# Retention into a gated feed-forward block on one core: a gap behind each head of v, and a new order of loads and transposes for chunks 2 and 3

## The chip, the cores and the metric

The kernel runs on one core of a Trainium2 chip. The metric is the device time in microseconds. TensorE (PE) multiplies matrices, VectorE (DVE), ScalarE (ACT) and GpSimd (POOL) work on elements, and SyncE (SP) issues transfers. POOL issues transfers too; both queues end on the same 16 DMA engines.

## The reference

Four batches of eight heads go through a retention recurrence, and its output, laid out as 3072 tokens of 512, through an RMS norm and a gated feed-forward block:

```
B, H, S, D = 4, 8, 768, 64
for t in range(S):
    state = gamma[h] * state + outer(k[:, :, t], v[:, :, t])
    y[:, :, t] = (1 / sqrt(D)) * q[:, :, t] @ state
x   = y.transpose(0, 2, 1, 3).reshape(B * S, H * D)
xn  = x / sqrt(mean(x * x) + 1e-6) * rms_g
out = (silu(xn @ w_gate) * (xn @ w_val)) @ w_out        # 512 -> 1536 -> 512
```

## The kernel before, in words

The 768 steps are cut into six chunks of 128. In a chunk, a **unit** is one batch: 128 steps on the partitions, eight heads of 64 in the free dimension; two units make a **pair**. The recurrence becomes matrix work: scores `a_ps` from the transposed k and q (`a_pe`, L485; `a_pair` does both units of a pair), a causal mask on DVE (`a_mask`, L494), values `y_ps` from masked scores and from the running state (`values`, L514 and L531), and the chunk's contribution to the state (`kv_ps`, L523; added on DVE by `state_add`). The decays are put on v beforehand (`vp`, L468, on POOL) and on y afterwards (`y_out`, L440, on DVE). Then come the squares (`square`, L449, on ACT), the inverse root (`rstd`, L454 and L370, on POOL), the norm (`norm`, L462, on DVE) and a transpose of the normed rows into `xnT`.

The feed-forward part of a chunk covers its 512 tokens: `gv` (L560) multiplies by the two input weights into PSUM, ACT takes the silu (L564), DVE the product `hT` (L565); `down` (L579) multiplies by the output weight, ACT copies to `o_sb` (L581), SP stores it. Chunks 0 and 1 use a layout of their own for the attention part (pairs of steps, `load_pair`, `tp`, `ap`, `y0`, `y1`, L300 for the weighting of v), and q and k are transposed on TensorE there. From chunk 2 on, `load` fetches q and k per unit as bf16 and v as float32, all on POOL's queue (L110 for v, L113 for q and k), and `t_dma` (L476) transposes q and k by DMA transposes on SP's queue. `x_dma` (L543) transposes the normed rows there too.

Everything is written out in program order by hand: each engine takes its instructions in that order. The feed-forward of chunk c runs on PE while the attention of chunk c + 1 is prepared and put between its steps; the table `after` says which calls follow which step. In chunk 1's stage there are 12 steps of `gv` and four of `down`: the attention of chunk 2 lies inside it, and the scores of chunk 3's first pair (`values(2, 1, (3, 0), True)`) close step 12. The loads and transposes of chunks 2 and 3 are placed in the last part of chunk 0's stage and in chunk 1's stage.

Tiles come in rings of buffers: v of a unit has 6 (`v_f`, shared with the four exponential masks of chunk 0, `mask0`), q and k 8 each, the transposed ones 8 each, output rows 3. A load into a ring waits until the last reader of the buffer is through.

Of the kernel before, what the change touches and what calls it, by code (L numbers as in the profile page):

```python
# [8 lines left out]
F32 = mybir.dt.float32  # L9
# [7 lines left out]
def kernel(  # L17
# [14 lines left out]
    B, H, S, D = q.shape  # L32
# [12 lines left out]
    work = ctx.enter_context(tc.tile_pool(name="work", bufs=4))  # L45
# [19 lines left out]
    def bank(name, dtype=F32, ffn=False, i=None):  # L65
        if i is None and split[0]:
            i = turn[ffn] % 4 + 4 * ffn
            turn[ffn] += 1
        elif i is None and first:
            i = first.pop(0)  # L70
        elif i is None:
            i = order[0]
            order.append(order.pop(0))
        return psum.tile([128, 512 if dtype == F32 else 1024], dtype, name=name, tag=f"p{i}")
# [30 lines left out]
    def load(c, b, names="qkv"):  # L105
        u = U.setdefault((c, b), {})
        for n in names:
            if n == "v":
                x = work.tile([128, H, D], F32, name="v_f", tag="v_f", bufs=6)
                nc.gpsimd.dma_start(out=x, in_=unit_v[n][c, b])  # L110
            else:
                x = work.tile([128, DM], BF16, name=n + "b", bufs=8)
                nc.gpsimd.dma_start(out=x.rearrange("p (h d) -> p h d", h=H), in_=unit_v[n][c, b])  # L113
            u[n] = x
# [58 lines left out]
    nc.vector.tensor_scalar(out=causal, in0=off, scalar1=0.0, scalar2=None, op0=ALU.is_ge)  # L173


    mask0 = [[work.tile([128, 2, 256], F32, name="mask0", tag="v_f", bufs=6) for i in range(2)] for a in range(2)]

    def mask_exp(a):
        for i in range(2):
# [103 lines left out]
    def ap_mask(c, p, a, i):  # L283
        u = U[c, p]
        am = work.tile([128, 2, 2, 128], BF16, name="am2", tag="am", bufs=12)
        m = mask0[a][i] if c == 0 else causal_p[:, None, :].to_broadcast([128, 2, 256])
        u["mask", a, i] = nc.vector.tensor_tensor(  # L287
            out=am.rearrange("p x e t -> p x (e t)"),
            in0=u["a_ps", a][i].rearrange("p (x t) -> p x t", x=2), in1=m, op=ALU.mult)
        u["am", a, i] = am  # L290
# [6 lines left out]
    def vp_pair(c, p):  # L297
        u = U[c, p]
        x = work.tile([128, H * 2, D], BF16, name="vp2", bufs=3)
        nc.gpsimd.tensor_tensor(  # L300
            out=x, in0=u["v"].rearrange("p h (e d) -> p (h e) d", e=2),
            in1=vd_p[:, c].rearrange("p h e -> p (h e)")[:, :, None].to_broadcast([128, 2 * H, D]), op=ALU.mult)
        u["vp"] = x.rearrange("p (h e) d -> p h (e d)", e=2)
# [99 lines left out]
    def y1(p):  # L403
        u = U[1, p]
        u["y"] = [bank("y_ps") for _ in range(2)]
        for b in range(2):
            for hp in range(NHP):
                nc.tensor.matmul(u["y"][b][:, hp * 128:(hp + 1) * 128],
                                 u["qT", hp // 2][b][:, hp % 2].rearrange("p e j -> p (e j)"), st_d[p][:, b, hp],
                                 start=hp == 0, stop=False, skip_group_check=True)  # L410
        for h in range(H):
            hp, i = h // 2, h % 2
            for e in range(2):
                for b in range(2):
                    r = slice(b * 64, b * 64 + 64)
                    nc.tensor.matmul(u["y"][b][:, h * D:h * D + D], u["am", hp // 2, i][r, hp % 2, e, :],
                                     u["vp"][r, h, e * D:e * D + D], start=False,
                                     stop=h == H - 1 and e == 1, skip_group_check=True)

    def y1_out(p):  # L420
        u = U[1, p]
        x = work.tile([128, 2, NHP, 2, D], F32, name="x", tag="x", bufs=2)
        u["x"] = x.rearrange("p b a i d -> p b (a i d)")
        for b in range(2):
            nc.vector.tensor_tensor(
                out=u["x"][:, b].rearrange("p (h d) -> p h d", h=H), in0=u["y"][b].rearrange("p (h d) -> p h d", h=H),
                in1=yd_p[:, :, None].to_broadcast([128, H, D]), op=ALU.mult)
# [16 lines left out]
    def square(c, p, b):  # L444
        u = pair(c, p)
        if b == 0:
            u["ms_"] = work.tile([128, 2], F32, name="ms", bufs=4)
        xsq = work.tile([128, DM], BF16, name="xsq", bufs=2)
        nc.scalar.activation(xsq, u["x"][:, b], AF.Square, scale=1.0 / math.sqrt(DM), accum_out=u["ms_"][:, b:b + 1])  # L449
# [7 lines left out]
    def norm(c, p, *units):  # L457
        u = pair(c, p)
        if 0 in units:
            u["xn"] = [work.tile([128, DM], BF16, name="xn", bufs=6) for _ in range(2)]  # L460
        for b in units:
            nc.vector.scalar_tensor_tensor(out=u["xn"][b], in0=u["x"][:, b], scalar=u["rstd"][:, b:b + 1], in1=g_bc,  # L462
                                           op0=ALU.mult, op1=ALU.mult)
# [8 lines left out]
    def t_dma(c, b):  # L472
        u = U[c, b]
        for n in "qk":
            t = work.tile([128, NHP, 128], BF16, name=n + "T", tag=n + "T", bufs=8)
            nc.sync.dma_start_transpose(out=t, in_=u[n])  # L476
            u[n + "T"] = t
# [70 lines left out]
    def gv(c, n0, n1, t0, t1):  # L548

        if c not in HT:  # L550
            HT[c] = work.tile([128, NFF, GT], BF16, name="hT", bufs=1)
        w = t1 - t0
        m = (n1 - n0) * w
        ps = []
        for wt, name in ((wg_b, "g_ps"), (wv_b, "v_ps")):
            x = bank(name, ffn=True)
            for n in range(n0, n1):
                o = (n - n0) * w
                for s in range(KS):
                    nc.tensor.matmul(x[:, o:o + w], wt[:, s, n * 128:(n + 1) * 128], XT[c][:, s, t0:t1],  # L560
                                     start=s == 0, stop=s == KS - 1)
            ps.append(x)
        sg = work.tile([128, 512], BF16, name="sg", bufs=4)
        nc.scalar.activation(sg[:, :m], ps[0][:, :m], AF.Silu)  # L564
        return nc.vector.tensor_tensor(  # L565
            out=HT[c][:, n0:n1, t0:t1], in0=sg[:, :m].rearrange("p (n t) -> p n t", t=w),
            in1=ps[1][:, :m].rearrange("p (n t) -> p n t", t=w), op=ALU.mult)

    def store(eng, c, b, m, o_sb):
        if c < 2:  # L570
            for e in range(2):
                eng.dma_start(out=out_e[c, b, e][:, m], in_=o_sb[e * 64:e * 64 + 64, m])
        else:
            eng.dma_start(out=out_v[c, b][:, m], in_=o_sb[:, m])

    def down(c, b):
        ps = bank("o_ps", ffn=True)
        for n in range(NFF):
            nc.tensor.matmul(ps, HT[c][:, n, b * C:(b + 1) * C], wo_b[:, n, :], start=n == 0, stop=n == NFF - 1)  # L579
        o_sb = work.tile([128, DM], F32, name="o_sb", bufs=3)  # L580
        nc.scalar.copy(o_sb, ps)  # L581
        store(nc.sync, c, b, slice(0, DM), o_sb)
# [122 lines left out]
    ap_mask(1, 0, 1, 1)  # L705
    state1(0)
    gv(0, 11, 12, 0, GT)
    load(2, 0)
    y1(0)
    down(0, 0)  # L710
    y1_out(0)
    square(1, 0, 0)
    square(1, 0, 1)
    rstd(1, 0)
    state_cast(0)
    norm(1, 0, 0, 1)
    load(2, 1)
    vp_pair(1, 1)
    load(2, 2)
    down(0, 1)  # L720
    down(0, 2)
    t_dma(2, 0)
    for n, e in (("q", "a"), ("k", "v")):
        tp1(1, n)
        tc1(1, n, e)
# [6 lines left out]
    for a in range(2):  # L732
        for i in range(2):
            ap_mask(1, 1, a, i)
    load(2, 3)
    t_dma(2, 1)
    down(0, 3)

    def run(steps, after):
        for i, step in enumerate(steps):  # L740
            step()
            for f in after.get(i, ()):
                f()

    def L(f, *a):
        return lambda: f(*a)
# [3 lines left out]
    steps += [L(down, 1, b) for b in range(B)]  # L750
    split[0] = True
    run(steps, {
        0: [L(y1, 1), L(y1_out, 1), L(kvp, 1, 1)],
        1: [L(square, 1, 1, 0), L(square, 1, 1, 1), L(rstd, 1, 1), L(state1, 1)],
        2: [L(begin, 2), L(norm, 1, 1, 0, 1), L(state_cast, 1), L(vp, 2, 0), L(vp, 2, 1), L(t_dma, 2, 2),
            L(t_dma, 2, 3)],
        3: [L(load, 3, 0, "qk"), L(load, 3, 1, "qk")],
        4: [L(x_pe, 1, 1, 0), L(x_copy, 1, 1, 0, "v"), L(x_pe, 1, 1, 1), L(x_copy, 1, 1, 1, "a"),
            L(load, 3, 0, "v"), L(load, 3, 1, "v")],
        5: [L(a_pair, 2, 0), L(a_mask, 2, 0, 0)],  # L760
        6: [L(a_mask, 2, 0, 1), L(a_mask, 2, 1, 0), L(vp, 2, 2), L(vp, 2, 3)],
        7: [L(a_mask, 2, 1, 1)],
        8: [L(values, 2, 0), L(y_out, 2, 0, 0), L(y_out, 2, 0, 1), L(state_add, 2, 0), L(load, 3, 2),
            L(t_dma, 3, 0), L(t_dma, 3, 1)],
        9: [L(square, 2, 0, 0), L(load, 3, 3)],
        10: [L(a_pair, 2, 1), L(square, 2, 0, 1), L(a_mask, 2, 2, 0), L(a_mask, 2, 2, 1), L(state_cast, 0),
             L(rstd, 2, 0)],
        11: [L(a_mask, 2, 3, 0), L(a_mask, 2, 3, 1), L(t_dma, 3, 2)],
# [7 lines left out]
    for c in range(2, NCH):  # L776
# [4 lines left out]
        d = c + 1  # L781
# [59 lines left out]
```

## Time and profile before

| | |
|---|---|
| median of 8 runs | 238.9 us (236.45 to 468.08) |
| profiled execution, its own time | 238.12 us |
| its span, first to last instruction | 236.3 us |
| PE busy | 226.0 us (96%) |
| DVE, ACT, POOL busy | 127.4, 87.6, 115.0 us |
| DMA packets, bytes | 83,307, 30.25 MB |
| chunk 1's stage, 59.1 to 98.4 us | PE busy 37.66 of 39.30, DMA share 1.85 |
| chunk 2's stage, 98.4 to 133.4 us | PE busy 34.84 of 35.00, DMA share 1.21 |
| chunk 3's stage, 133.4 to 168.2 us | PE busy 34.64 of 34.80, DMA share 1.21 |

Busy time says how long an engine had work, not what set the end. The DMA share is the summed time of all packets over 16 engines; it can exceed 1, since packets of one engine overlap. In the profile q0 is POOL's queue of transfers and q1 SP's. A row of a timeline gives start, length, engine, line, operation and tiles, and in brackets the idle time before it with what ended that. One of the eight runs, 468.08 us, stands far from the others, which lie between 236.45 and 240.17.

### The profile page before, as it was taken

Reading aid. Unit: us, or ns where it says so; the run is one execution under the profiler, and the core shown is the slowest. Engines: PE = TensorE matmul, PEld = TensorE weight load, DVE = VectorE, ACT = ScalarE, POOL = GpSimd, SP = SyncE. Lnnn points to the kernel's source line nnn. Section 1 sums busy time; section 2 is a strip of 40 time slices with the busy share of each in tenths; the row PEclk is TensorE's granted clock in tenths of the full one; section 3 lists DMA queues with packets and bytes.
Section 4 is the critical chain, followed back from the end, with each engine's and each line's share of the span. In section 5 each row is a group of like instructions: output and inputs, shape, how many; then the busy total and the mean of one; then the engine's idle time right before and its main releaser. Section 6 shows DMA issues by size and latency. Waiting matters only on the chain.

```text
span 236.3 us, 5541 instructions
## 1 busy us (share of the span) xinstructions
PE 226.0 (96%) x2268; PEld 138.4 (59%) x2290; DVE 127.4 (54%) x222; ACT 87.6 (37%) x176; POOL 115.0 (49%) x150
## 2 busy tenths in 40 slices
PE   7987999999999997999999999999999999999994
PEld 2455785545898863684454684454674544864443
DVE  3775644827486688246967046967155742234300
ACT  2865634242443423225323235332325241333211
POOL 8976799669599925942927703917001000000000
PEclk9999999999999999999999999999999999999999
DMA  8999999999999999999993999992540204200022
GB/s 105 164 189 203 188 173 178 198 190 246 150 170 149 183 138 204 99 220 174 103 125 25 173 169 213 112 113 68 135 111 0 47 0 141 84 0 0 3 90 89
DMA packets 83307, 30.25 MB, mean 128 GB/s; under 512 B 69521, under 2 KB 78993, under 8 KB 83282
## 3 DMA queue, kind: packets, MB, share of 16 engines
q0 software_dynamic: 51328, 16.52, 75.2%
q1 hardware_dynamic: 31280, 13.25, 30.2%
q8 instruction: 18, 0.29, 0.5%
q10 hardware_dynamic: 674, 0.14, 0.3%
q14 instruction: 7, 0.06, 0.1%
HBM read 28.32 MB, written 6.29 MB: 146 GB/s over the span
## 4 chain that ended last, share of the span: by engine, by line
PE 85%; DMA 8%; DVE 3%; issue 1%; ACT 1%; POOL 1%; DVEq 0%; POOLq 0%
PE v_ps L560 25%; PE o_ps L579 24%; PE g_ps L560 24%; DMA kT<-kb 4%; DMA wv_b<-in_moe_w_val_dram 3%; PE hot L219 3%; PE a_ps L485 1%; PE y_ps L514 1%; DVE am L287 1%; PE o_ps L590 1%; PE y_ps L531 1%; PE kv_ps L523 1%; PE a_ps L280 1%; PE kv_ps L329 1%; PE t_ps L234 1%
## 5 line engine op out<-in xcount | busy, mean ns | idle before, releaser
L565 DVE TENSOR_TENSOR hT<-sg,v_ps 128x512 bf16<-128x512 bf16 (+1 forms) x76 | 49.9, 658 | 76.9 <-PE v_ps L560 67.4
L560 PE MATMUL v_ps<-xnT,wv_b 128*128 128x256 bf16 (+1 forms) x427 | 74.9, 309 | 1.3 <-DMA wv_b<-in_moe_w_val_dram 1.0
L560 PE MATMUL g_ps<-xnT,wg_b 128*128 128x256 bf16 (+1 forms) x417 | 73.8, 308 | 1.2 <-DMA wg_b<-in_moe_w_gate_dram 0.6
L564 ACT ACTIVATE sg<-g_ps 128x512 bf16<-128x512 f32 (+1 forms) x76 | 43.6, 574 | 76.3 <-PE g_ps L560 71.9
L579 PE MATMUL o_ps<-wo_b,hT 128*128 128x512 bf16 x269 | 60.6, 379 | 0.4
L560 PEld LDWEIGHTS <-wv_b 128*128 128x128 bf16 x428 | 41.7, 98 | 22.2 <-DMA wv_b<-in_moe_w_val_dram 1.6
L560 PEld LDWEIGHTS <-wg_b 128*128 128x128 bf16 x428 | 40.4, 98 | 21.5 <-DMA wg_b<-in_moe_w_gate_dram 0.9
L579 PEld LDWEIGHTS <-hT 128*128 128x128 bf16 x276 | 26.5, 98 | 31.7
L454 POOL TENSOR_SCALAR m<-ms 128x2 f32<-128x2 f32 x10 | 2.2, 219 | 70.5 <-ACT xsq L449 70.4
L581 ACT COPY o_sb<-o_ps 128x512 f32<-128x512 f32 x23 | 13.4, 584 | 46.4 <-PE o_ps L579 41.3
L462 DVE SCALAR_TENSOR_TENSOR xn<-x,rstd,g_bc 128x512 bf16<-128x512 f32 x20 | 19.5, 1004 | 9.2 <-POOL rstd L370 9.2
L494 DVE TENSOR_TENSOR am<-a_ps,causal 128x512 bf16<-128x512 f32 x32 | 21.1, 682 | 0.0
L468 POOL TENSOR_TENSOR vp<-v_f,vd_n 128x512 bf16<-128x512 f32 x16 | 19.4, 1236 | 0.0
L449 ACT ACTIVATE xsq<-x 128x512 bf16<-128x512 f32 x20 | 12.4, 623 | 9.3 <-DVE x L440 9.3
L113 POOL DMA_DIRECT2D qb<-in_q_dram x16 | 15.1, 943 | 0.6 <-DMA wo_b<-in_moe_w_out_dram 0.6
L113 POOL DMA_DIRECT2D kb<-in_k_dram x16 | 14.4, 898 | 1.8 <-DMA wo_b<-in_moe_w_out_dram 1.8
L110 POOL DMA_DIRECT2D v_f<-in_v_dram x16 | 14.7, 921 | 0.0
L440 DVE TENSOR_TENSOR x<-y_ps,yd_n 128x512 f32<-128x512 f32 x16 | 10.6, 685 | 1.7 <-PE y_ps L531 1.7
L219 PE MATMUL hot<-ones 128*128 128x512 bf16 x25 | 9.6, 503 | 1.5 <-DVE ones L146 1.4
L300 POOL TENSOR_TENSOR vp<-v2f,vd_p 128x1024 bf16<-128x1024 f32 x4 | 7.7, 1928 | 0.1
L370 POOL TENSOR_TENSOR rstd<-m,mhalf 128x2 f32<-128x2 f32 x10 | 7.2, 718 | 0.8
L485 PE MATMUL a_ps<-qT,kT 64*128 64x128 bf16 x128 | 5.1, 217 | 1.5 <-DMA kT<-kb 1.5
(96 smaller groups left out, 155.2 us busy)
## 6 DMA issues: line engine op xcount, KB each, us to landing
v_f<-in_v_dram POOLq DMA_DIRECT2D x16, 256.0 KB, 7.0
out_dram<-o_sb SPq DMA_DIRECT2D x15, 256.0 KB, 2.4
out_dram<-o_sb SPq DMA_DIRECT2D x17, 128.0 KB, 5.6
qb<-in_q_dram POOLq DMA_DIRECT2D x16, 128.0 KB, 6.0
kb<-in_k_dram POOLq DMA_DIRECT2D x16, 128.0 KB, 6.6
wg_b<-in_moe_w_gate_dram POOLq DMA_DIRECT2D x6, 256.0 KB, 8.0
wv_b<-in_moe_w_val_dram POOLq DMA_DIRECT2D x6, 256.0 KB, 8.5
wo_b<-in_moe_w_out_dram POOLq DMA_DIRECT2D x3, 512.0 KB, 9.2
```

The costliest lines, as they stand in the source:

```text
L110: nc.gpsimd.dma_start(out=x, in_=unit_v[n][c, b])
L113: nc.gpsimd.dma_start(out=x.rearrange("p (h d) -> p h d", h=H), in_=unit_v[n][c, b])
L219: nc.tensor.matmul(hot, ones[:, :128], ones, start=True, stop=True)
L449: nc.scalar.activation(xsq, u["x"][:, b], AF.Square, scale=1.0 / math.sqrt(DM), accum_out=u["ms_"][:, b:b + 1])
L462: nc.vector.scalar_tensor_tensor(out=u["xn"][b], in0=u["x"][:, b], scalar=u["rstd"][:, b:b + 1], in1=g_bc, op0=ALU.mult, op1=ALU.mult)
L468: nc.gpsimd.tensor_tensor(out=x, in0=U[c, b]["v"], in1=vd_n[:, c, :, None].to_broadcast([128, H, D]), op=ALU.mult)
L494: nc.vector.tensor_tensor(out=x, in0=u["a_ps"][i].rearrange("p (a t) -> p a t", a=NHP), in1=causal[:, None, :].to_broadcast([128, NHP, 128 ...
L560: nc.tensor.matmul(x[:, o:o + w], wt[:, s, n * 128:(n + 1) * 128], XT[c][:, s, t0:t1], start=s == 0, stop=s == KS - 1)
L564: nc.scalar.activation(sg[:, :m], ps[0][:, :m], AF.Silu)
L565: return nc.vector.tensor_tensor(out=HT[c][:, n0:n1, t0:t1], in0=sg[:, :m].rearrange("p (n t) -> p n t", t=w), in1=ps[1][:, :m].rearrange( ...
L579: nc.tensor.matmul(ps, HT[c][:, n, b * C:(b + 1) * C], wo_b[:, n, :], start=n == 0, stop=n == NFF - 1)
L581: nc.scalar.copy(o_sb, ps)
```

## The change

Three things are altered.

1. The tile that a unit's v is loaded into gets eight unused elements behind each head of 64, so that a head's 256 bytes no longer touch the next head's. The masks that share the ring take the same tile shape and use its first 512 elements as before.
2. q and k of chunk 2's units are loaded ahead of the v's: q and k of unit 1 move up beside those of unit 0, and the v's follow later, behind the weighting of chunk 1's second pair. For chunk 3, q and k of units 0 and 1 move from step 3 to step 0 of chunk 1's stage, those of units 2 and 3 from steps 8 and 9 to step 6; the v's stay where they were.
3. The DMA transposes of chunk 2's unit 0 move from behind `down(0, 2)` to behind `down(0, 0)`, those of unit 1 from ahead of `down(0, 3)` to behind `down(0, 1)`.

```diff
@@ load
-                x = work.tile([128, H, D], F32, name="v_f", tag="v_f", bufs=6)
+
+                x = work.tile([128, H, D + 8], F32, name="v_f", tag="v_f", bufs=6)[:, :, :D]
                 nc.gpsimd.dma_start(out=x, in_=unit_v[n][c, b])
@@ masks of chunk 0
-    mask0 = [[work.tile([128, 2, 256], F32, name="mask0", tag="v_f", bufs=6) for i in range(2)] for a in range(2)]
+    mask0 = [[work.tile([128, H, D + 8], F32, name="mask0", tag="v_f", bufs=6) for i in range(2)] for a in range(2)]
+    mask0 = [[m.rearrange("p h d -> p (h d)")[:, :512].rearrange("p (x t) -> p x t", x=2) for m in ms] for ms in mask0]
@@ end of chunk 0's stage
     gv(0, 11, 12, 0, GT)
-    load(2, 0)
+    load(2, 0, "qk")
+    load(2, 1, "qk")
     y1(0)
     down(0, 0)
+    t_dma(2, 0)
     y1_out(0)
     square(1, 0, 0)
     square(1, 0, 1)
     rstd(1, 0)
     state_cast(0)
     norm(1, 0, 0, 1)
-    load(2, 1)
     vp_pair(1, 1)
-    load(2, 2)
+    load(2, 0, "v")
+    load(2, 2, "qk")
+    load(2, 1, "v")
+    load(2, 3, "qk")
     down(0, 1)
+    t_dma(2, 1)
     down(0, 2)
-    t_dma(2, 0)
...
-    load(2, 3)
-    t_dma(2, 1)
+    load(2, 2, "v")
+    load(2, 3, "v")
     down(0, 3)
@@ chunk 1's stage, after these steps
-        0: [L(y1, 1), L(y1_out, 1), L(kvp, 1, 1)],
+        0: [L(y1, 1), L(y1_out, 1), L(kvp, 1, 1), L(load, 3, 0, "qk"), L(load, 3, 1, "qk")],
...
-        3: [L(load, 3, 0, "qk"), L(load, 3, 1, "qk")],
         4: [L(x_pe, 1, 1, 0), ...
             L(load, 3, 0, "v"), L(load, 3, 1, "v")],
...
-        6: [L(a_mask, 2, 0, 1), L(a_mask, 2, 1, 0), L(vp, 2, 2), L(vp, 2, 3)],
+        6: [L(a_mask, 2, 0, 1), L(a_mask, 2, 1, 0), L(vp, 2, 2), L(vp, 2, 3),
+            L(load, 3, 2, "qk"), L(load, 3, 3, "qk")],
-        8: [..., L(load, 3, 2), ...
+        8: [..., L(load, 3, 2, "v"), ...
-        9: [L(square, 2, 0, 0), L(load, 3, 3)],
+        9: [L(square, 2, 0, 0), L(load, 3, 3, "v")],
```

More of the change, by code (lines that the diff above doesn't have):

```diff
@@ L760 @@
         5: [L(a_pair, 2, 0), L(a_mask, 2, 0, 0)],
-        6: [L(a_mask, 2, 0, 1), L(a_mask, 2, 1, 0), L(vp, 2, 2), L(vp, 2, 3)],
+        6: [L(a_mask, 2, 0, 1), L(a_mask, 2, 1, 0), L(vp, 2, 2), L(vp, 2, 3),
+            L(load, 3, 2, "qk"), L(load, 3, 3, "qk")],
         7: [L(a_mask, 2, 1, 1)],
-        8: [L(values, 2, 0), L(y_out, 2, 0, 0), L(y_out, 2, 0, 1), L(state_add, 2, 0), L(load, 3, 2),
+        8: [L(values, 2, 0), L(y_out, 2, 0, 0), L(y_out, 2, 0, 1), L(state_add, 2, 0), L(load, 3, 2, "v"),
             L(t_dma, 3, 0), L(t_dma, 3, 1)],
-        9: [L(square, 2, 0, 0), L(load, 3, 3)],
+        9: [L(square, 2, 0, 0), L(load, 3, 3, "v")],
         10: [L(a_pair, 2, 1), L(square, 2, 0, 1), L(a_mask, 2, 2, 0), L(a_mask, 2, 2, 1), L(state_cast, 0),
```

## The prediction

> **What bounds the kernel now.** I read the page first (busy shares, the chain that ended last), then the waits by engine, then the chain inside chunk 1's stage, and last the transfers there.
>
> ```profile
> PE 226.0 (96%) x2268; PEld 138.4 (59%) x2290; DVE 127.4 (54%) x222; ACT 87.6 (37%) x176; POOL 115.0 (49%) x150
> PE 85%; DMA 8%; DVE 3%; issue 1%; ACT 1%; POOL 1%; DVEq 0%; POOLq 0%
> ...
> PE a_ps L485 <- DMA kT<-kb: 1.5, 1, 1.5
> ...
> PE v_ps L560 <- DMA wv_b<-in_moe_w_val_dram: 1.0, 1, 1.0
> PE g_ps L560 <- DMA wg_b<-in_moe_w_gate_dram: 0.6, 1, 0.6
> ```
>
> TensorE is busy for 226.0 of 236.3 us, and the page's row of granted clocks is 9 in all 40 slices. The diff leaves the order on PE, ACT and DVE as it is; it moves work on POOL's and SP's queues alone. So a gain can only come out of PE's waits. The two for weights lie before 24 us, ahead of the change. What is left is one wait of 1.53 us, for the transposed k of chunk 3:
>
> ```profile
> 78.81 1.17 DVE x L440 x2
> 79.98 10.27 DMA kT<-kb
> 90.25 0.05 issue
> 90.29 0.40 PE a_ps L485 x8
> ...
> 88.37 0.39 PE L485 MATMUL a_ps<-qT,kT 64*128 64x128 bf16 x8
> 90.29 0.40 PE L485 MATMUL a_ps<-qT,kT 64*128 64x128 bf16 x8 [1.53 <-DMA kT<-kb]
> ```
>
> The first group is the chain between 58 and 100 us (start, length, what), the second PE's timeline there. The last transpose of units 0 and 1 of chunk 3 is issued at 79.98 and lands 10.27 us later, at 90.25; PE stood from 88.76. Why it took 10.27 us is seen in the transfers from 78.2 to 80.8 us, against those from 65 to 67.5:
>
> ```profile
> DMA packets 469, 0.56 MB, mean 215 GB/s; under 512 B 342, under 2 KB 342, under 8 KB 469
> q0 software_dynamic: 467, 0.56, 122.2%
> q1 hardware_dynamic: 2, 0.00, 0.1%
> ...
> q0 software_dynamic: 1236, 0.16, 96.3%
> q1 hardware_dynamic: 921, 0.23, 71.5%
> ```
>
> In the first stretch two v units pass on POOL's queue (q0) in 127 packets of 4 KB (469 less 342), and SP's queue (q1) gets two packets, though transposes issued at 77.33, 78.68 and 79.98 wait there. In the second, q0 carries q and k in 128-byte packets, and the transposes get 921. So v in large packets shuts out the transposes; q and k share.
>
> **The change part by part.**
>
> *The order of loads.* POOL issues a unit's q, k or v in about 0.9 us. Now q and k of chunk 3's units 0 and 1 are issued from 69.76 to 73.35, behind the weighting of v (L468). They move to step 0 of the stage. POOL's way there: between 44.70 and the end of chunk 2's last v load (61.65 + 0.94 = 62.59) it keeps the same instructions, but the q and k of unit 1 (0.94 + 0.88 = 1.82) move into the idle 1.99 us before L454 at 51.12. The weighting of chunk 1's second pair (L300, 1.93 us) moves from 55.38 to 52.67 and must wait there for v2f, issued at 42.03 and 11.1 us on its way (53.1): +0.4. So the eleventh and twelfth loads end near 62.59 - 1.82 + 0.4 = 61.2, and the four of chunk 3 (0.99 + 0.89 + 0.89 + 0.90 = 3.67) near 64.9, some 8 us earlier than now. They do not land 8 us earlier, since q0 is busy all that time: DMA share is 1.85 of 16 engines from 59.1 to 98.4. The bounds are no gain and 8 us; I take 3 to 4, because only the gap in which q0 had nothing issued (kb of unit 3 lands at 71.8, the next issue is 69.76 and lands at 75.1) and the two v's no longer ahead fall away. The last transpose would then be issued near 76.5 instead of 79.98.
>
> *v in 256-byte elements.* A 4 KB packet took 301 ns (79.2 to 80.7 us: 106.2% of 16 engines, 99 packets, nearly all of them v), four per engine and unit: 1.20 us. The trace has no uncast 256-byte packet on q0. The nearest rows are q1's transposes, 256 bytes each: 18.5 ns alone (94 to 96 us, 60.0% for 1040 packets), 31 ns when q0 is busy too (921 packets above). 64 per engine: 1.18 to 1.99 us. A unit costs between 0.02 us less and 0.79 more of an engine's time; in the crowded stage I take the upper third, +0.6. Four v's stand ahead of chunk 3's q and k (units of chunk 2): 2.4 us back from the gain in landing. What it buys is that transposes run beside v as beside q and k: 2.6 us of shut-out at 78.2 vanish from a transpose's 10.27. Net: issue near 78, flight 7 to 8 us, landing 85 to 86 against the 88.76 at which PE asks. **The 1.53 us go: -1.53.** If the cover of 2.8 us is gone, the wait comes back, up to its present size.
>
> [...]
>
> *Chunk 2's transposes behind the first two stores.* On SP, t_dma(2,0) goes from behind the third pair of stores (56.14) to behind the first (51.5); it waits for qb, landing 44.70 + 9.1 = 53.8. The stores of down(0,1), ready at 52.34, queue behind two transposes of 1.2 to 1.35 us, some 4 us late. Nobody waits: an output tile has three buffers, and its next writer there, down(0,3)'s copy at 59.34, uses the buffer of the first store. PE asks for chunk 2's transposes at 71.62; now the last is issued at 61.53 and flies 9.0 us (70.5), 1.1 us of cover. Earlier issue widens it. Cost 0.
>
> *Strided reads.* L468 reads v through the gap, 16 times 1.10 us. The nearest row is a cast, 0.60 us dense (L348) and 0.68 strided (L345): 0 to 0.08 us each, POOL has room: 0. The masks keep their layout.
>
> *New waits on POOL.* At 44.70 and 47.36 POOL stood for wo_b:
>
> ```profile
> 44.70 0.91 POOL L113 DMA_DIRECT2D qb<-in_q_dram  x1 [0.62 <-DMA wo_b<-in_moe_w_out_dram]
> 47.36 0.88 POOL L113 DMA_DIRECT2D kb<-in_k_dram  x1 [1.75 <-DMA wo_b<-in_moe_w_out_dram]
> ...
> 65.33 0.22 POOL L454 TENSOR_SCALAR m<-ms 128x2 f32<-128x2 f32 x1 [2.74 <-ACT xsq L449]
> ```
>
> Each waits for the load eight before it (wo_b issued at 35.19 and 35.92). After the change, the k of chunk 3's unit 1 is eight behind the v of chunk 2's unit 1, issued near 57.6. That v lands by the rows of v in 4.8, 7.0 or 11.1 us (shortest, median, longest): 62.4, 64.6 or 68.7. With 0.9 for the issue, L454 (now 65.33) would start 0, 0.2 or 4.3 us late. Behind it stand rstd, the state's cast and L468 on POOL, and on DVE the two L462 at 66.72 with the hT's of two steps behind them. PE's cover: rstd ends 0.4 us before DVE takes L462, whose second ends at 68.91, and PE's x_ps asks for it near 69.7: 1.2 us. I take the value between median and longest that a fuller queue gives, 1.5 us late, so **+0.3**. L468's readers, at 77.4, are far off.
>
> *Later chunks.* SP's transposes and loads stay in order. One cover is thin: the x_dma issued at 129.42 flies 8.2 us to 137.6, and PE's g_ps asks at 138.00. v's come with it on q0; the gap lets it through sooner (gain, PE does not wait) or adds packets (0.4 us are covered). 0.
>
> **Sum**: 238.12 (the profiled execution; span 236.3 and 1.8 around it) - 1.53 + 0.3 = 236.9. The median of the runs shown is 238.9, 0.8 above the profiled one, and the fastest undisturbed run, 236.45, is where the profiled one would be with no wait at all (236.6): I read the spread partly as this wait being longer or shorter. I write 236.9, 0.8% under the median.
>
> **Rivals.**
>
> A, the forecast: the wait goes, new ones cost 0 to 0.5. 235.8 to 238.2. Chance 0.62.
>
> B, slower: POOL's eight-deep line. From 2.7 us late on (1.2 of cover plus the 1.53 gained) it decides. With the longest v flight and two v's 0.8 us longer each by the upper price, L454 comes 5.9 us late: PE stands 4.7, and the time is 236.6 + 4.7 = 241.3; with the longest flight alone, 3.1 of standing, 239.7. For it: kb of chunk 2's unit 3 took 11.0 us in this very queue. Against it: the v of unit 1 took 6.6, and the loads ahead of it are the same number as now. Typical 240.5. Chance 0.20.
>
> C, it does not do what it says: packets stay at 4 KB, since v's source runs are already 256 bytes, or the crowded queue returns what the order gains, and kT lands near 90 again. 238.1 to 239. For it: the DMA share; against it: the two packets in 2.6 us. Chance 0.18.
>
> **How the numbers follow.** 1% of the median, 2.4 us, is about what a measurement of this kernel can tell from no change. A crosses it only where the unprofiled runs wait longer than 1.53 us, as the median suggests: 0.36 faster, 0.26 within. B: 0.13 slower, 0.07 within. C: 0.01 faster, 0.13 within, 0.04 slower. Sum 0.37, 0.46, 0.17. The range runs from a little under A's low end to B's typical time, 235.6 to 240.4.
>
> **What would show it.** Right: PE's list of waits has no kT; the queue lines show some 15,400 more packets (1,024 of 4 KB become 16,384 of 256 B); in stretches where v passes, q1 has hundreds of packets; L454 stays within 1.2 us of 65.3. Wrong: PE waiting for x_ps or v_ps at 69 to 71 us (B); unchanged packet counts (C); a wait for transposes at 71.6.

## The result, and the profile after

| | before | after |
|---|---|---|
| median of all runs | 238.82 us (59 runs) | 245.77 us (22 runs, 239.01 to 1310.81) |
| ratio after / before | | 1.0088, 95% interval 1.0048 to 1.0128 |
| profiled execution, its span | 238.12, 236.3 us | 245.32, 243.6 us |

The ratio here, and every ratio below, compares only the runs within 1.5% of each kernel's fastest one, of the changed kernel 6 of 22 and not the profiled one, which lies near the median; so the medians of all runs stand beside it, and the account below is one of the profiled execution. By both, the changed kernel is slower, by 0.9% in the ratio and 2.9% in the medians, where 236.9 was forecast and 235.6 to 240.4 given as the range.

The page of the kernel after: busy times, the row of granted clocks in 40 slices, the packets.

```profile
PE 228.3 (94%) x2268; PEld 139.2 (57%) x2290; DVE 129.1 (53%) x222; ACT 87.6 (36%) x176; POOL 115.0 (47%) x150
...
PEclk9999999999999996899999999999999999999999
...
DMA packets 83307, 30.25 MB, mean 124 GB/s; under 512 B 69521, under 2 KB 78993, under 8 KB 83282
```

Two things stand out. The packets are the 83,307 of before, to the last one: the gap behind each head has not made 256-byte packets out of v's 4 KB ones. And the clock, 9 in every slice before, falls to 6 and 8 in two slices, at 91 to 104 us.

PE's timeline there, after and then before:

```profile
88.89 0.39 PE L487 MATMUL a_ps<-qT,kT 64*128 64x128 bf16 x8
95.61 0.61 PE L487 MATMUL a_ps<-qT,kT 64*128 64x128 bf16 x8 [6.33 <-DMA kT<-kb]
96.15 0.61 PE L581 MATMUL o_ps<-wo_b,hT 128*128 128x512 bf16 x1
96.98 8.77 PE L581 MATMUL o_ps<-wo_b,hT 128*128 128x512 bf16 x34 [0.22 <-issue]
105.59 1.04 PE L562 MATMUL g_ps<-xnT,wg_b 128*128 128x256 bf16 x8
```

```profile
90.62 7.94 PE L579 MATMUL o_ps<-wo_b,hT 128*128 128x512 bf16 x35
98.40 1.04 PE L560 MATMUL g_ps<-xnT,wg_b 128*128 128x256 bf16 x8
```

The wait that should have gone has grown from 1.53 to 6.33 us. Behind it PE is slower too: from the scores to the first `g_ps` it takes 105.59 - 95.61 = 9.98 us, before 98.40 - 90.29 = 8.11. The windows of after give the granted clock (the third number from the end), then DMA share and GB/s:

```profile
86.00:89.00 3.00, 3.00 (x61) 1.96 (x61) 2.61 (x5) 0.58 (x1) 0.00 (x0) 1.00 1.75 123
92.00:95.00 3.00, 0.00 (x0) 0.00 (x0) 2.24 (x3) 0.00 (x0) 2.92 (x5) 0.62 1.42 141
95.00:98.00 3.00, 2.17 (x12) 1.08 (x14) 1.75 (x3) 0.00 (x0) 3.00 (x3) 0.50 1.07 263
98.00:101.00 3.00, 3.00 (x12) 1.15 (x10) 0.00 (x0) 0.39 (x1) 3.00 (x5) 0.74 1.44 115
```

So 7.3 us of span (243.6 - 236.3) are made up of 4.80 of wait (6.33 - 1.53), 1.87 of slower clock (9.98 - 8.11) and 0.52 by which PE came later to this point (88.89 against 88.37): 7.2. The 0.52 were there before chunk 1's stage, which begins at 59.62 instead of 59.10; behind this place 0.1 us is left over.

The chain of work around it, after:

```profile
81.10 14.46 DMA kT<-kb
95.56 0.05 issue
95.61 0.61 PE a_ps L487 x6
```

The last transpose of chunk 3's first pair is issued at 81.10 (before 79.98) and flies 14.46 us (before 10.27). So the 4.80 of wait are 1.12 of later issue and 4.19 of longer flight, less the 0.52 by which PE asked later. POOL had issued what it waits for long before:

```profile
62.23 0.96 POOL L114 DMA_DIRECT2D qb<-in_q_dram  x1
...
64.84 0.98 POOL L114 DMA_DIRECT2D kb<-in_k_dram  x1
65.89 0.22 POOL L456 TENSOR_SCALAR m<-ms 128x2 f32<-128x2 f32 x1
```

Issue and landing of the loads concerned, read off the transfers of both traces:

| chunk 3 | before | after |
|---|---|---|
| q, k of unit 0 | 69.8 to 75.1, 70.7 to 77.3 | 62.2 to 74.9, 63.1 to 77.7 |
| q, k of unit 1 | 71.6 to 78.6, 72.5 to 79.5 | 64.0 to 79.4, 64.8 to 81.0 |
| v of units 0, 1 | 73.3 to 80.7, 74.2 to 81.9 | 70.3 to 81.8, 71.3 to 82.8 |
| v of units 2, 3 | 78.9 to 87.7, 81.5 to 92.5 | 80.0 to 94.6, 81.5 to 95.4 |

Issued 7.6 us sooner, they land at about the same time (unit 0) or 0.8 to 1.5 us later (unit 1). q and k of units 2 and 3, issued 2.7 to 3.8 us sooner, land 0.9 to 2.8 us later. What the queues carried (packets, MB, share) from 70 to 73 us, before and then after:

```profile
q1 hardware_dynamic: 1512, 0.54, 110.4%
q0 software_dynamic: 52, 0.10, 12.2%
```

```profile
q1 hardware_dynamic: 561, 0.32, 84.2%
q0 software_dynamic: 765, 0.11, 66.3%
```

Before, POOL's queue (q0) had next to nothing there, and SP's (q1), with transposes and stores, ran by itself. Now the early loads fill this stretch, and SP's queue moves little more than a third of its packets. From 78 to 90.25 us, where the last transpose of before landed, before and then after:

```profile
q0 software_dynamic: 4944, 1.42, 164.0%
q1 hardware_dynamic: 2178, 0.52, 36.9%
```

```profile
q0 software_dynamic: 4774, 1.20, 120.2%
q1 hardware_dynamic: 2104, 0.50, 52.8%
```

Here both queues move about what they moved before, and over the last transpose's own flight SP's queue moves 201 packets a us, before 212. So it is not held off over the whole of it; a slow stretch stands out near the end. From 88 to 92 us the engines move 379 packets of q0 and 259 of q1 in the changed kernel (before 1,314 and 362), while v's of units 2 and 3 and the last transposes are under way. The v's and the last transpose land together, from 94.6 to 95.6 us.

### The profile page after: what moved, and what is told of

Its sections match the earlier page's. It is cut to its first block, busy times and chain, and to the rows that moved or that the text cites. A ratio compares the mean times of both kernels' runs of the same rounds, so it can differ in the third digit from the quotient of the medians.

```text
span 243.6 us, 5540 instructions
## 1 busy us (share of the span) xinstructions
PE 228.3 (94%) x2268; PEld 139.2 (57%) x2290; DVE 129.1 (53%) x222; ACT 87.6 (36%) x176; POOL 115.0 (47%) x150
## 2 busy tenths in 40 slices
DMA packets 83307, 30.25 MB, mean 124 GB/s; under 512 B 69521, under 2 KB 78993, under 8 KB 83282
## 4 chain that ended last, share of the span: by engine, by line
PE 82%; DMA 9%; DVE 5%; issue 1%; POOL 1%; ACT 1%; DVEq 0%; POOLq 0%
PE v_ps L562 24%; PE g_ps L562 23%; PE o_ps L581 22%; DMA kT<-kb 6%; DMA wv_b<-in_moe_w_val_dram 3%; PE hot L221 3%; PE a_ps L487 2%; DVE xn L464 1%; PE y_ps L516 1%; DVE am L289 1%; PE o_ps L592 1%; PE y_ps L533 1%; PE kv_ps L525 1%; PE a_ps L282 1%; PE t_ps L236 1%
## 5 line engine op out<-in xcount | busy, mean ns | idle before, releaser
L562 PE MATMUL v_ps<-xnT,wv_b 128*128 128x256 bf16 (+1 forms) x427 | 74.9, 309 | 1.1 <-DMA wv_b<-in_moe_w_val_dram 0.7
L581 PE MATMUL o_ps<-wo_b,hT 128*128 128x512 bf16 x269 | 62.0, 386 | 0.5 <-issue 0.2
L581 PEld LDWEIGHTS <-hT 128*128 128x128 bf16 x276 | 27.0, 99 | 33.0 <-issue 2.4
L464 DVE SCALAR_TENSOR_TENSOR xn<-x,rstd,g_bc 128x512 bf16<-128x512 f32 x20 | 21.3, 1092 | 9.3 <-POOL rstd L372 9.3
L470 POOL TENSOR_TENSOR vp<-v_f,vd_n 128x512 bf16<-128x512 f32 x16 | 19.4, 1233 | 0.0
L487 PEld LDWEIGHTS <-kT 64*128 64x128 bf16 x128 | 3.8, 96 | 8.2 <-DMA kT<-kb 6.5
```

The source lines that it names most:

```text
L470: nc.gpsimd.tensor_tensor(out=x, in0=U[c, b]["v"], in1=vd_n[:, c, :, None].to_broadcast([128, H, D]), op=ALU.mult)
L487: nc.tensor.matmul(ps[i][:, hp * 128:(hp + 1) * 128], u["kT"][r, hp, :], u["qT"][r, hp, :], start=True, stop=True)
```

## The experiments

The change has four parts that can be taken apart: the gap, the move of chunk 3's first two q/k to step 0, that of the second two to step 6, and chunk 2's part (loads and transposes). The theory after the result: the move to step 0 alone makes the loss, through the crowd it joins. The edits are shown shortened. The rivals: the gap (longer v's), POOL's eight-deep line (B of the prediction), or the sum of all parts.

**The gap alone (e1), chunk 3's moves alone (e2), chunk 2's part alone (e3), the change without step 6 (e4).**

```diff
 e1:  v_f: [128, H, D]  ->  [128, H, D + 8][:, :, :D], masks alike; order as before
 e2:  0: [..., + L(load, 3, 0, "qk"), L(load, 3, 1, "qk")]
      6: [..., + L(load, 3, 2, "qk"), L(load, 3, 3, "qk")]; v dense
 e3:  end of chunk 0's stage as after; chunk 3 and v as before
 e4:  after, but L(load, 3, 2), L(load, 3, 3) whole at steps 8 and 9
```

> The kernel before with the gap behind each head of v alone. Theory 1 (the gap changes no packet; what lengthens PE's wait for kT is the moved loads): 83,307 packets as before, 4 KB packets still there, PE's wait for kT near 1.5 us, time within 0.4% of before. Rival (writing through a gap slows the transfers of v): the v units take longer to land than the median 7.0 us of before, PE waits 4 us or more, time up 1% or more.

> The kernel before with the moves of chunk 3's q and k alone (units 0 and 1 at step 0, units 2 and 3 at step 6), no gap, chunk 2 as before. Theory 1 (the moved loads of chunk 3 fill the stretch in which chunk 2's transposes ran alone, and overlay their own transposes): PE waits for kT 4 to 6 us, time up about 1 to 3%. Rival (chunk 2's new order is the cause): PE's wait stays at 0 to 2 us, time within 0.5% of before.

> The kernel before with chunk 2's part alone: q and k of unit 1 beside those of unit 0, the v's later, transposes behind the first two stores; no gap, chunk 3 as before. Theory 1: PE's wait for kT of chunk 3 is 0 to 1.5 us, as chunk 2's transposes are done sooner; time 0 to 0.6% under before. Rival (chunk 2's new order is the cause of the loss): wait of 4 us or more, time up 1% or more.

> The changed kernel with q and k of chunk 3's units 2 and 3 put back to steps 8 and 9; all else as changed. Theory 1a (it is those four loads, issued at 74 to 79 us, that lie over the transposes of units 0 and 1): the wait for kT falls from 6.3 us to under 1.5, time 236.5 to 238. Theory 1b (the early loads of units 0 and 1 do the harm, by filling the stretch where chunk 2's transposes ran alone): the wait stays at 4 us or more, time as of the changed kernel.

| | median of all (before 239.93) | ratio | PE's waits for kT |
|---|---|---|---|
| e1 | 243.91 (4 runs) | 1.0150 [1.0024, 1.0277] | 1.66, 1.23, 3.79 |
| e2 | 243.48 (4 runs) | 1.0198 [1.0083, 1.0312] | 1.17, and 1.05 twice for x_ps |
| e3 | 242.90 (10 runs) | 1.0016 [0.9943, 1.0088] | 1.78 |
| e4 | 243.76 (4 runs) | 1.0195 [1.0087, 1.0303] | 1.97, 3.18 |

Chunk 2's part costs nothing that the ratio shows, and e13 below, which holds it too, shows none either. In the profiled executions of e1, e3 and e4 the granted clock is halved for 3.4 us near 22 to 26 us (e3: 22.4 to 25.9), and chunk 1's stage begins at 61.55, 61.19 and 61.79 instead of 59.10. That lies ahead of every transfer that was moved, and the changed kernel, with all these edits, has none there; so it is not put down to them. Step 6 is not needed for the loss (e4), nor is the gap (e2). e1 left the gap open: four runs, an interval that reaches from nothing to 3%, and the same 83,307 packets. In e2 the kT wait was to be 4 to 6 us and was 1.17; there rival B shows itself. PE's timeline, with POOL's `m` of chunk 1 late behind a wait of 2.0 us for an earlier k:

```profile
70.73 0.40 PE L390 MATMUL x_ps<-ident,xn 128*128 128x128 bf16 x4 [1.05 <-DVE xn L462]
72.18 0.44 PE L390 MATMUL x_ps<-ident,xn 128*128 128x128 bf16 x4 [1.05 <-DVE xn L462]
```

**The price of v by packet (e5).** Three v's and three transposes issued together in the last stage, where no other load runs, for dense float32 v, v with gaps, and v written as bf16.

```diff
+ x = dense / gapped float32, or bf16;  nc.gpsimd.dma_start(out=x, in_=unit_v["v"][0, r])   # three
+ nc.sync.dma_start_transpose(out=t, in_=U[NCH - 1, r]["q"])                                # three
```

> The kernel before with three extra bursts in the last chunk's feed-forward stage, where its own transfers are idle: three v units loaded on POOL's queue and three transposes issued on SP's at the same moment, first with v dense in its tile, then with a gap of 256 bytes behind each head, then with v cast to bf16. Nothing reads them. Theory (the gap does not change how v travels, and 4 KB packets shut out the transposes either way): dense and gap both show 192 packets of 4 KB, their v's land within 0.5 us of each other, the transposes beside them fly equally long, 4 to 7 us; beside bf16 v, 3,072 packets of 128 bytes, the transposes fly 1 us or more shorter. Rival (a write through a gap is dearer): the 4 KB packets of the gap take 10% or more longer and its v's land 0.5 us or more later each.

From issue to landing, v took 4.46, 5.48, 6.08 us dense, 4.87, 6.46, 6.52 with gaps and 4.04, 4.85, 5.52 as bf16; the whole burst 8.44, 8.98 and 7.53 us. Dense and gapped v both went in 192 packets of 4 KB for three units (mean 317 and 319 ns), the bf16 one in 3,072 of 128 bytes. The gap here was 256 bytes, in the kernel 32. The transposes beside flew 4.5 and 5.8 us (dense, two of the three read), 4.5 to 6.6 (gap) and 3.6 to 5.3 (bf16), which is less than the 1 us of difference that was expected. Each burst ran once, so half a microsecond more for the gap is not a finding; the packets are.

**Only step 0 (e9), only step 6 (e10), the new order without the gap (e8).**

```diff
 e9:  before, 0: [..., + L(load, 3, 0, "qk"), L(load, 3, 1, "qk")], step 3 empty
 e10: before, 6: [..., + L(load, 3, 2, "qk"), L(load, 3, 3, "qk")], 8, 9: "v" only
 e8:  after, with v_f dense as before
```

> The kernel before with q and k of chunk 3's units 0 and 1 at step 0 instead of step 3, nothing else. Theory 3 (issued earlier they only queue longer: POOL's queue is full there, the stretch in which chunk 2's last transposes ran alone is filled, so kT of unit 1 lands no sooner): kb of unit 1 lands within 1.5 us of the 79.5 of before or later, PE's wait for kT stays at 1 us or more, and POOL's wait for its eighth load back delays L454 by 1 us or more; median 0 to 3 us over before. Rival (the early issue helps, the loss comes from units 2 and 3): the wait is under 0.5 us, median 0.5 to 1.5 us under before.

> The kernel before with q and k of chunk 3's units 2 and 3 at step 6 instead of steps 8 and 9, their v's where they were, nothing else. Theory 3 (loads placed beside the transposes of units 0 and 1 lengthen their flight): kT of unit 1 flies 12 us or more instead of 10.3, PE waits 2.5 to 5 us, median 1 to 5 us over before. Rival (POOL is still busy with the weighting of units 2 and 3, so the loads leave hardly earlier): wait 1 to 2 us, median within 0.5% of before.

> The changed kernel without the gap. Theory (the moved loads make the loss): as the changed kernel, PE waits for kT 3 to 6 us, median 3 to 7 us over before. Rival (the gap makes the loss): the wait is 0 to 1.5 us and the median within 1.5 us of before.

e9: median 244.00 (6 runs; before 238.82), ratio 1.0222 [1.0149, 1.0296]. e10: 238.85 (12 runs), 1.0018 [0.9978, 1.0057]; the theory gave it a flight of 12 us and a wait of 2.5 to 5, its rival 1 to 2 us of wait and the time of before. The last transpose flew 7.4 us, PE did not wait for it, and the time was that of before. e8: 244.36 (6 runs; before 238.74), 1.0205 [1.0147, 1.0263], a kT wait of 4.78 us. The move of q and k of units 0 and 1 makes the loss by itself. POOL's `m`, expected 1 us late or more, was 0.9 late (66.23 against 65.33). PE's timeline of e9:

```profile
90.25 0.40 PE L485 MATMUL a_ps<-qT,kT 64*128 64x128 bf16 x8 [1.32 <-DMA kT<-kb]
93.86 0.61 PE L485 MATMUL a_ps<-qT,kT 64*128 64x128 bf16 x8 [3.21 <-DMA kT<-kb]
94.40 5.95 PE L579 MATMUL o_ps<-wo_b,hT 128*128 128x512 bf16 x17
```

The k of unit 1, issued at 65.2, landed at 81.7 (before 72.5 and 79.5): the same picture as after, with no other edit.

**v as bf16 (e7).** The order of before; v of units converted on its way, which takes its 4 KB packets away (98,667 packets).

```diff
-                x = work.tile([128, H, D], F32, name="v_f", tag="v_f", bufs=6)
+                x = work.tile([128, H, D], BF16, name="v_h", bufs=6)
```

> The kernel before with a unit's v loaded as bf16, so in 128-byte packets as q and k; v is rounded before its weighting instead of behind it. Theory (the 4 KB packets of v shut out the transposes): stretches in which v passes show hundreds of packets on SP's queue, kT of chunk 3's unit 1 lands 2 us sooner, PE's wait goes, time 0.3 to 1% under before. Rival (many small packets cost the crowded stage more than they free): the wait grows past 2 us and the time rises by 0.5% or more.

237.70 (12 runs, none over 239.9; before 238.74), ratio 0.9971 [0.9939, 1.0002]; PE still waits 1.04 us for kT, where none was expected. This is in the direction of the theory, but too small to call faster. And its hundreds of packets on SP's queue are not there everywhere. From 79 to 81 us, with a transpose issued at 76.57 under way, the queues carried this, and nothing on q1:

```profile
q0 software_dynamic: 2359, 0.30, 283.3%
```

So beside packets of 128 bytes too the transposes went 2 us without one.

**The whole change without the move to step 0 (e13), and the whole new order with v as bf16 (e16).** These two decide.

```diff
 e13: after, but L(load, 3, 0, "qk"), L(load, 3, 1, "qk") at step 3 as before
 e16: after's order with all its moves; v_f replaced by e7's bf16 tile, no gap
```

> The changed kernel whole, but with q and k of chunk 3's units 0 and 1 left at step 3. Theory 1 (the move to step 0 is the cause, everything else in the change is harmless): no PE wait for kT over 2 us, full granted clock after 85 us, median within 1% of before (238 to 240). Theory 2 (gap, step 6 and chunk 2's part add up to the loss, the move to step 0 only tips it): a kT wait of 3 us or more and a half-clock stretch remain, median 242 to 245.

> The whole new order, step 0 too, but without the gap and with the v of units written as bf16 (their packets are then 128 bytes, none of 4 KB). If the early loads lose because v's 4 KB packets shut the transposes out, the kT wait falls under 1 us and the median is 237 to 239. If they lose because of the crowd of loads ahead, whatever the packets, kT lands at 93 or later, the wait stays 3 to 6 us and the median 242 to 245.

e13: 238.84 (12 runs; before 239.11), ratio 1.0005 [0.9965, 1.0045], PE waits 1.87 us for kT. The gap, step 6 and chunk 2's part are together worth nothing; without the move to step 0 no loss is left.

e16: 238.42 (10 runs, the longest 240.48), ratio 0.9984 [0.9939, 1.0030]. Step 0 is in it, and the loss is gone. PE's timeline:

```profile
89.52 0.41 PE L531 MATMUL y_ps<-st_b,qT 64*128 64x64 bf16 x16
89.77 0.61 PE L485 MATMUL a_ps<-qT,kT 64*128 64x128 bf16 x16
```

The last transpose flies 8.1 us (80.0 to 88.1) instead of 14.46, and the scores of both units run without a break. The early loads gain little here too: those of unit 0 land at 74.4 and 76.1, 0.7 and 1.2 us sooner than before. So at the scores the early loads lose only together with v in float32. The expectation that the crowd alone, whatever its packets, would keep the wait at 3 to 6 us fell.

| ratio to before | q, k of units 0, 1 at step 3 | at step 0 |
|---|---|---|
| v float32 (4 KB packets) | e1 1.0150, e3 1.0016, e6 1.0036, e10 1.0018, e13 1.0005 | after 1.0088, e2 1.0198, e4 1.0195, e8 1.0205, e9 1.0222, e12 1.0272 |
| v bf16 (128 bytes) | e7 0.9971, e11 1.0288, e15 0.9991 | e16 0.9984 |

e1 has four runs and the wide interval given above; e11 and e12, described below, lose at another place. e16's v also moves fewer bytes (28.16 MB in all against 30.25) and no longer shares its buffers with chunk 0's masks; neither was taken apart from the size of its packets.

**Do two queues lose by running together (e14)?** In the last stage: four q loads alone, four transposes alone, then four of each at once.

```diff
+ nc.gpsimd.dma_start(out=x.rearrange(...), in_=unit_v["q"][1, r])            # four, bursts 1 and 3
+ nc.sync.dma_start_transpose(out=t, in_=U[NCH - 1, r]["k"])                  # four, bursts 2 and 3
```

> Kernel before with three probe bursts in the last stage, where no other load runs: four q loads alone, four transposes alone, then four loads and four transposes issued together. If the two queues only share the engines' time, the mixed burst takes at most the sum of the two alone and each transpose flies up to twice as long (alone some 4.5 to 6 us by an earlier burst of three). If mixing itself loses throughput, the mixed burst takes clearly longer than the sum. The time of the whole, 237 to 241, matters little.

Loads alone took 7.2 us from first issue to last landing (205.91 to 213.12), transposes alone about 6 (212.61 to the last packets near 218.5), both together 9.2 (219.51 to 228.67), well under the sum. The queues in the second and the third burst:

```profile
q1 hardware_dynamic: 2176, 0.52, 37.8%
```

```profile
q0 software_dynamic: 4160, 0.52, 92.4%
q1 hardware_dynamic: 2309, 0.77, 42.6%
```

Beside loads in 128-byte packets (4,160 of them) the queues together lost nothing here, 9.2 us against 7.2 and 6; but a transpose that flew 2.4 us alone flew 3.9 to 6.0.

**Ways to a faster kernel (e6, e11, e12, e15).** e6 puts the loads of units 2 and 3 of chunk 3 later, e11 does so with v as bf16, e12 in the changed kernel; e15 is e7 with step 6.

```diff
 e6:  load(3, 2), load(3, 3): q, k behind step 11, v behind vp(3, 1); t_dma(3, 2), (3, 3) behind the x_dma's
 e11: e7 + the late loads, t_dma(3, 2) at step 11, t_dma(3, 3) between x_dma(2, 0, 1) and x_dma(2, 1, 0)
 e12: after + the same late loads and transposes as e11
 e15: e7 + e10
```

> The kernel before with the loads of chunk 3's units 2 and 3 later: q and k behind step 11 instead of 8 and 9, the v's behind the weighting of units 0 and 1, their transposes behind the normed rows' transposes. Theory (what lies on POOL's queue beside the transposes of units 0 and 1 sets when kT lands): kT of unit 1 lands 3 to 6 us sooner, PE's wait for it goes, the median falls by 1.5 to 3 us, fewer runs with a clock under 0.99. Rival (the queues are full whatever the order): the wait stays at 1 us or more and the time is that of before.

> A version meant to beat both: the kernel before with v of a unit loaded as bf16, q and k of chunk 3's units 2 and 3 behind step 11, their v's behind the weighting of units 0 and 1, and their transposes ahead of the normed rows' second pair. Theory: PE waits neither at chunk 3's first pair nor at its second; 236.0 to 237.2 in the median, 0.6 to 1.2% under before, no run over 241. Rival (another transfer takes the place of the one relieved, as the second pair's did when the units were only moved): a wait of 1 us or more for kT or xnT, time within 0.5% of before.

> The changed kernel, gap and all, with the loads of chunk 3's units 2 and 3 placed late as in the version meant to beat both. Theory 3 (the loads beside the transposes make the long wait): PE's wait for kT of the first pair falls from 6.3 us to under 1, median 237 to 239. Rival (the early q and k of units 0 and 1, or chunk 2's order, are enough to make it): the wait stays at 2 us or more, median 241 or more.

> The kernel before with v of units as bf16 and q, k of chunk 3's units 2 and 3 at step 6; nothing at step 0. Theory 1: no kT wait, 236.5 to 238, ratio 0.992 to 0.998, faster than either part alone by at most 0.5 us. Theory 2 (any earlier load costs): a kT wait of 2 us or more and over 240.

e6: 239.95 (12 runs; before 238.74), 1.0036 [0.9998, 1.0075]: the last transpose flew 4.1 us and PE did not wait for it, but 1.74 us for the next pair's at 109.45. e11: 244.84 (6 runs; before 238.82), 1.0288 [1.0226, 1.0350]; e12: 245.35 (6 runs), 1.0272 [1.0203, 1.0341]. All three were expected to be faster than what they altered. In e11 and e12 the kT wait is gone, and one for the normed rows' transposes stands 4.52 (e11) and 6.51 us (e12), because transposes put ahead of them on SP's queue hold them (e11: SP stands 6.1 us for a q, and the last two are issued at 99.4 and 101.8, before 93.5 and 95.0). e12 has the move to step 0 and v in float32, and yet the last transpose of chunk 3's first pair flies 5.2 us (83.3 to 88.5). So the long flight takes a third thing, the loads and transposes of units 2 and 3 beside it. e15: 238.23 (12 runs; before 239.11), 0.9991 [0.9959, 1.0022], no kT wait, but not the gain over e7 that was expected. No version is surely faster than before; e7 comes nearest.

## Why the prediction was wrong, step by step

**What bounds the kernel: right.** The time hung on the one kT wait; no other place moved by more than 0.5 us.

**The order of loads: the issue times right, the landing wrong. This step failed.** POOL's four loads were to end near 64.9; they ended at 65.8. "I take 3 to 4" us of gain at the landing; measured, the landings moved by -0.2 and +0.4 us for unit 0 and by +0.8 and +1.5, which is later, for unit 1. The last transpose was issued at 81.10, not at 76.5, or "near 78" with the price of v (76.5 and 2.4 make 78.9). The bounds themselves, "no gain and 8 us", left out a loss: the same trace showed that in the old order transposes of chunk 2 ran in the gap of q0 ahead of 73 us, by themselves. The early loads fill that gap. e14 shows what company on q0 cost a transpose (2.4 us alone, 3.9 to 6.0 beside loads), and e9 that this one move is enough for the loss. To fill the gap is not enough by itself, since e16 fills it too, with 1,262 packets of q0 and 888 of q1 from 70 to 73 us, and loses nothing.

**v in 256-byte elements: the edit without effect, the mechanism half right.** That float32 v has to do with the loss is confirmed: e16 has none where e8 has 1.0205, with the reservations made above. But "q and k share" is not the rule. In e7 2,359 packets of 128 bytes passed from 79 to 81 us without one of q1, and in the kernel before 1,210 from 74 to 75 us, with a transpose issued at 71.88 under way. So it is not shown that the size of the packets is what holds transposes up. The price of 301 ns per 4 KB packet comes out over the 83 packets of that size alone; the other 16 of the 99 are small. But the 15,400 packets more never came, so the first half of rival C was true. The destination's layout did not decide the packet here: e5 had 192 of 4 KB for three units either way, and 3,072 of 128 bytes where v was converted to bf16 on its way. What sets the size of a packet no run shows.

**The flight, 7 to 8 us: measured 14.46. This step failed too, and it is the larger part.** Against the forecast the transpose was issued some 3 us late and flew 6.5 to 7.5 us longer, so it landed at 95.56 instead of 85 to 86. The forecast rested on smaller packets, which did not come; in e16, where v did go in 128-byte packets, the flight was 8.1. With the packets unchanged the loads of both pairs stood in one stretch, and in e12, where those of the second pair come later, the flight was 5.2 us. The present 10.27 us were not the worst case: the term of -1.53, with a wait that would come back "up to its present size", became +4.80.

**The clock: a term that the sum did not have.** 1.87 us come with PE at half clock behind the long wait, from 95.6 to 99.5 us. Rival B, with 4.7 us of standing, left such a term out too.

**Chunk 2's transposes, 0: right** (e3 1.0016; kT of unit 1 landed at 69.3, before 70.5). **Strided reads, 0: right** (L470 1,233 ns, L468 before 1,236). **POOL's eight-deep line, +0.3:** `m` started 0.56 us later (65.89 against 65.33), within the cover, so 0 on the path after: PE's `x_ps` starts at 69.85 without a wait. In e2 it did reach PE, with 1.05 us twice.

**The rivals.** The forecast (0.62) failed. B (0.20) named the right sign and the wrong place. C (0.18) had both mechanisms, packets that stay and a crowded queue, but priced them at no change: it let the queue return what the order gains, not more than that. That rival should have had a slower end, with a longer flight than the present one and the clock behind it.

## What to carry to other kernels

Loads issued 7.6 us earlier into a queue that was busy all along landed no more than 0.2 us earlier here, and up to 1.5 us later. So look in the trace for what runs in the pause that an early load will fill. The size of a transfer's packets is a thing to count in the trace, not to infer from the layout of a tile: here they were 83,307 with the gap and without. And when a forecast allows for a wait on TensorE, price the clock behind it as well: the 6.33 us here came with 1.87 more.

## What the runs showed of the hardware

Waits and clock. After: 6.33 us of wait, half clock from 92.7 to 99.5 us. e9: 1.32 and 3.21 us of wait within 5 us, half clock for 6.8 us. Every trace with a wait of 3 us or more there has such a stretch behind it: 3.4 us in e11, 6.8 in after, e1, e4, e8 and e9, 10.2 in e12. e2: twice 1.05 us within 2.5 us, half clock for 3.4 us. Single waits of 1.53 (before), 1.74 (e6), 1.78 (e3) and 1.87 us (e13): none there. The stretches were 3.4, 6.8 and 10.2 us long. What makes the clock fall, and for how long, no run shows: e2 had its stretch with no single gap over 1.1 us.

What stays open: why transposes move next to no packet for 2 us and more, beside 4 KB packets (127 of these against two in the 2.6 us that the prediction shows) and beside those of 128 bytes (2,359 against none in 2 us of e7); by what float32 v makes the early loads lose, its packets, its bytes or something else; and why from 88 to 92 us in the changed kernel the engines moved only 379 packets of q0 and 259 of q1, while transposes and v's were under way. The experiments show which edits together make the loss; by what mechanism the last transpose comes to fly 14.46 us they do not show.
